# A Fourier-mixing network: products with 33 and 64 contraction rows are given all 128

## The chip, the cores and the metric

The kernel runs on one core of one Trainium2 chip. The metric is the device time of one execution in microseconds, the median of several runs, and a profile was taken of one execution. TensorE (PE) does matrix products, VectorE (DVE), ScalarE (ACT) and GpSimd (POOL) the element-wise work, and SyncE (SP) issues the transfers (DMA). A product loads one operand as weights (PEld, LDWEIGHTS) and streams the other; the number of *rows* of a product is the number of partitions over which it contracts, its *columns* are the partitions of its output, and its width is the number of elements streamed.

## The reference

Eight batches of 576 tokens with 512 features. Attention makes x, a block with a two-dimensional Fourier transform mixes it and runs a feed-forward net, and a second net with token shift follows.

```python
# attention, per batch and head
q_s = softmax(q, axis=-1); k_s = softmax(k, axis=2)
x = einsum(q_s, einsum(k_s, v))                 # 8 x 576 x 512
# first net
X = np.fft.fft(np.fft.fft(x, axis=1), axis=2)
u = x + np.real(X)
un = (u - mean(u)) / np.sqrt(var(u) + 1e-06)
x = u + np.maximum(un @ w_ch1, 0.0) @ w_ch2
# second net
x_prev = shifted by one token
k = np.maximum((mu_k*x + (1-mu_k)*x_prev) @ w_k, 0.0)
v = k * k @ w_v
out = sigmoid((mu_r*x + (1-mu_r)*x_prev) @ w_r) * v
```

## The kernel before

**Stages.** The tokens of all batches form one sequence of 4608, cut into nine blocks of 512. For block `i` the products of the first net run as `mm1` (L938, into the PSUM tile `h`) and `mm2` (L959, into `acc`), with each f32 operand split into a high and a low f16 part. Between them, `side()` takes one step each of two strands: `front_x` (attention of the next batches) and `front_y` (the transform and the normalization of the next batches). So the transform of batch 0 runs before the first block, the transforms of batches 1 to 7 run between the main products of the blocks, on the same PE queue, and end at about 855 us; after the ninth block the second net runs (L1002, L1015, L1030). A scheduler sets the order in which each engine's instructions are queued; each engine runs its queue in order.

**The transform** of a batch is two stages of products in `fp32r`, each operand split in a high and a low part.

In stage 1 (L469 to L488) six groups of products form `yh` and `yl`: for i = 0, 1, 2 and e = 0 (cosine) or 1 (sine). `JT` gives the output columns: 128, 128 and then 64 (e = 0) or 32 (e = 1). A group is six products with 128 rows (L477); the three groups with e = 0 end in a seventh (L480), whose operands `x6` and `alt` have 33 partitions. Only partitions 0 and 32 hold data: the high and the low part of one row.

In stage 2 (`stage2`, L493) a group is six products with 128 rows (L497) and a last one (L501). The three groups a batch with the cosine table `csh`, `csl` have one more before the last, L499, over the first 64 partitions. In the third slice of `yh` partitions 0 to 63 hold the high part of the remaining rows and 64 to 127 their low part; `csl[:, 2]` is zero from partition 64 on. The last product has 128 rows with the cosine table and 96 with the sine table `ssh`.

So a batch has three products with 33 rows (two with 128 columns, one with 64) and three with 64 rows, 24 of each in the kernel. After each L480 group ACT and DVE take the result to `yh` and `yl`; after each cosine group of stage 2 ACT copies it to `pc` (L507) or `sd` (L517).

**The start.** `first_constants` loads the table `alt` (33 x 290) through a staging tile `st` of tag `pc`, of which there is one buffer, and copies it by ACT to `alt` and to `x6` (L147). The buffer held 1/512 before, which ACT reads at L142. Attention of batch 0 follows on the same queues; its maximum (DVE, L304), the exponentials of q (ACT, L327) and k (ACT, L334) and the products with v (PE, L345) are named below. The f16 weights are decoded meanwhile on DVE (L194, L195).

Of the kernel before, what the change touches and what calls it, by code (L numbers as in the profile page):

```python
# [8 lines left out]
F32 = mybir.dt.float32  # L9
F32R = mybir.dt.float32r  # L10
# [11 lines left out]
NS = 290  # L22
# [21 lines left out]
def net(ctx, tc, q, k, v, w1, w2, mu_k, mu_r, w_k, w_v, w_r, ce_d, se_d, cs_d, ss_d, alt_d, id_d, out):  # L44
    nc = tc.nc
# [13 lines left out]
    def bank(tag, bufs, shape=(128, 512)):  # L59
        return ps.tile(list(shape), F32, tag=tag, name=tag, bufs=bufs)  # L60
# [3 lines left out]
    def aside(first, strand):  # L64


        turn_of[0] += 1
        if not first:
            return bank(f"side{turn_of[0] % 2 if done_block[0] < 0 else strand}", 1)
        x = turn_of[0] % 6  # L70
        return bank(f"side{x // 3}", 1) if x in (0, 3) else bank(f"acc{(1, 2, 4, 5).index(x)}", 1)

    mm = nc.tensor.matmul
# [19 lines left out]
    fc = front.enter_context(tc.tile_pool(name="fc", bufs=1))  # L93
    fw = front.enter_context(tc.tile_pool(name="fw", bufs=1))
# [25 lines left out]
    csl = fc.tile([128, 3, NS], F32R, name="csl")  # L120
    ssh = fc.tile([128, 3, NS], F32R, name="ssh")
    ssl = fc.tile([128, 3, NS], F32R, name="ssl")
    alt = fc.tile([33, NS], F32R, name="alt")
    x6 = fc.tile([33, NS], F32R, name="x6")
    kvbd = [fc.tile([128, 2, 129], F32, name=f"kvbd{x}") for x in range(2)]

    def load_constants():
# [9 lines left out]
    def first_constants():  # L137
        st = fw.tile([128, NS], F32, tag="pc", name="st")[:, 0:128]
        nc.vector.memset(st, 1.0 / DM)
        nc.vector.memset(one, 1.0)  # L140
        nc.gpsimd.memset(wsc[:, 7:8], 1e-6)
        nc.scalar.activation(out=onesr, in_=st, func=AF.Copy)  # L142
        nc.sync.dma_start(out=ident, in_=id_d)
        st = fw.tile([128, NS], F32, tag="pc", name="st")[0:33]
        nc.sync.dma_start(out=st, in_=alt_d)
        for x in (alt, x6):
            nc.scalar.activation(out=x, in_=st, func=AF.Copy)  # L147
        for x in kvbd:
            nc.gpsimd.memset(x, 0.0)
# [136 lines left out]
    def attention(b):  # L286
        tt = nc.vector.tensor_tensor
        for hf in range(2):
            if (b, hf) == (0, 0):
                load_k(b, 0)  # L290
                load_q(b, 0)
                first_constants()
                load_k(b, 1)
                load_v(b, 0)
                load_q(b, 1)
                load_v(b, 1)
# [119 lines left out]
    def transform(b):  # L416
# [50 lines left out]
        yh = fw.tile([128, 3, NK + 256], F32R, tag="yh", name="yh")  # L467
        yl = fw.tile([128, 3, NK + 256], F32R, tag="yl", name="yl")
        for i in range(3):  # L469
            for e, (ch, cl, n0, n1) in enumerate(((ceh, cel, 0, NK), (seh, sel, NK, NK + 256))):  # L470
                j0, n = JT[e][i]
                js = slice(j0, j0 + n)
                pt = aside(b == 0, 1)[0:n, 0:n1 - n0]
# [19 lines left out]
        def stage2(cols, ch, cl):  # L493
            pt = aside(b == 0, 1)[:, 0:NS]
            for i in range(2):
                for a, c in ((yh, ch), (yh, cl), (yl, ch)):
                    mm(out=pt, lhsT=a[:, i, cols], rhs=c[:, i, :], start=(i == 0 and c is ch and a is yh), stop=False)  # L497
            if ch is csh:
                mm(out=pt, lhsT=yh[0:64, 2, cols], rhs=cl[0:64, 2, :], start=False, stop=False)  # L499
            n = 128 if ch is csh else 96  # L500
            mm(out=pt, lhsT=yh[0:n, 2, cols], rhs=ch[0:n, 2, :], start=False, stop=True)  # L501
            return pt

        for g in range(2):
            pp = stage2(slice(1 + 128 * g, 129 + 128 * g), csh, csl)
            pc = fw.tile([128, NS], F32, tag="pc", name="pc")
            nc.scalar.activation(out=pc, in_=pp, func=AF.Copy)  # L507
            yield 1
            qq = stage2(slice(NK + 128 * g, NK + 128 * g + 128), ssh, ssl)
            tt(out=sd[:, g, 1, :], in0=pc, in1=qq, op=ALU.subtract)  # L510
            tt(out=sd[:, g, 0, :], in0=pc, in1=qq, op=ALU.add)
            yield 1
        tt(out=u[:, 0:2, 0:289], in0=u[:, 0:2, 0:289], in1=sd[:, :, 1, 0:289], op=ALU.add)
        tt(out=u[:, 0:2, S - 1:288:-1], in0=u[:, 0:2, S - 1:288:-1], in1=sd[:, :, 0, 1:288], op=ALU.add)
        pp = stage2(slice(0, 128), csh, csl)
        nc.scalar.activation(out=sd[0:1, 0], in_=sd[0:1, 1], func=AF.Copy)
        ma = nc.scalar.activation(out=sd[0:1, 1], in_=pp[0:1, None, :].to_broadcast([1, 2, NS]), func=AF.Copy)  # L517
# [472 lines left out]
    for i, (t0, n) in enumerate(blocks):  # L990
# [7 lines left out]
        for x, (o, m) in enumerate(subs):  # L998
            pt = bank("h", 2)
# [145 lines left out]
def build(inputs):  # L1145
    import concourse.bacc as bacc

    nc = bacc.Bacc("TRN2", target_bir_lowering=False, num_devices=1, dynamic_dma_scratch_size=1024)
    arrays, args = {}, []
    for name, a in [*_laid_out(inputs).items(), *_constants().items()]:  # L1150
        arrays[f"in_{name}_dram"] = a
        args.append(nc.dram_tensor(f"in_{name}_dram", a.shape, mybir.dt.from_np(a.dtype), kind="ExternalInput").ap())
    b, _, s, _ = inputs["q"].shape
    args.append(nc.dram_tensor("out_0_dram", (b * s, DM), F32, kind="ExternalOutput").ap())
    with tile.TileContext(nc, schedule_with_timeline_sim=True) as tc:
        net(tc, *args)
    return nc, arrays
# [9 lines left out]
```

## Time and profile before

| | us |
|---|---|
| median of 3 runs | 1571.76 (1570.62 to 1573.12) |
| the profiled execution | 1570.43 |
| its span, first to last instruction | 1568.7 |
| PE busy with products | 1459.4 (93%) |
| DVE busy | 945.9 (60%) |
| ACT busy | 649.5 (41%) |
| POOL busy | 234.9 (15%) |

The span is the time between the first and the last instruction of the profiled execution, and 1.7 us of its time lie around it. Products overlap in PE's pipeline: each one's duration reaches into the next one's, so what a product takes of the queue is read from the difference of two starts, not from its duration. The granted clock is the share of TensorE's full clock (2.4 GHz) that it was given in a stretch: 1.00, or 0.50 for 1.2 GHz; a stretch of both shows a value between.

### The profile page before, as it was taken

How to read it: one execution, taken by the hardware profiler on the slowest of the kernel's cores; microseconds unless marked ns; L12 is line 12 of the kernel's file. 1: busy time of each engine (PE TensorE's matmuls, PEld its weight loads, DVE VectorE, ACT ScalarE, POOL GpSimd, SP SyncE). 2: the span in 40 equal slices, each digit the busy share in tenths (PEclk: the TensorE clock that was granted, in tenths of full speed). 3: DMA queues.
4: the chain of work that ended last, by engine and by line, in shares of the span. 5: the costliest groups of instructions: out<-in, count | busy, mean ns of one | idle time of the engine just before them, and what ended most of it. 6: DMA issues, size and time to landing. Idle time of an engine off the chain costs nothing.

```text
span 1568.7 us, 18474 instructions
## 1 busy us (share of the span) xinstructions
PE 1459.4 (93%) x7123; PEld 759.2 (48%) x7123; DVE 945.9 (60%) x1635; ACT 649.5 (41%) x1183; POOL 234.9 (15%) x183
## 2 busy tenths in 40 slices
PE   4547995899999999999999999997999999999999
PEld 3435653555555555555555444443444444444444
DVE  8897738646567585664542364777886556554423
ACT  5677523323334233332321243435665435543322
POOL 2653402111001020110200200221100000000000
PEclk9668996999999999999999999998999999999999
DMA  7651202101112111111011035431111011100000
GB/s 298 195 152 48 80 16 74 48 32 48 42 48 75 35 46 42 48 36 40 1 37 41 32 116 182 133 99 63 54 55 54 1 54 54 55 1 28 27 27 28
DMA packets 43988, 99.81 MB, mean 64 GB/s; under 512 B 5723, under 2 KB 12156, under 8 KB 43900
## 3 DMA queue, kind: packets, MB, share of 16 engines
q1 hardware_dynamic: 43900, 98.63, 18.6%
q8 instruction: 56, 0.92, 0.3%
q14 instruction: 32, 0.26, 0.1%
HBM read 79.73 MB, written 18.87 MB: 63 GB/s over the span
## 4 chain that ended last, share of the span: by engine, by line
PE 75%; DVE 16%; ACT 4%; issue 2%; DMA 2%; POOL 1%; DVEq 0%; ACTq 0%; POOLq 0%; SPq 0%
PE h L938 22%; PE acc L959 22%; PE h L1015 11%; PE acc L1030 8%; PE h L1002 3%; DVE aa L782 2%; PE side L497 2%; PE side L477 2%; DVE wr L195 2%; PE side L398 1%; PE side L345 1%; DVE wr L194 1%; DVE x L784 1%; ACT aa L778 1%; DVE m L304 1%
## 5 line engine op out<-in xcount | busy, mean ns | idle before, releaser
L938 PE MATMUL h<-unh,wr 128*128 128x512 f16 (+1 forms) x1216 | 372.5, 370 | 7.0 <-ACT wr L232 3.6
L959 PE MATMUL acc<-hh,wr 128*128 128x512 f16 x1152 | 367.0, 380 | 0.0
L938 PEld LDWEIGHTS <-wr 128*128 128x128 f16 x1824 | 175.8, 98 | 197.5 <-issue 11.8
L959 PEld LDWEIGHTS <-wr 128*128 128x128 f16 x1728 | 164.7, 98 | 192.3 <-issue 3.5
L938 PE MATMUL h<-unl,wr 128*128 128x512 f16 (+1 forms) x608 | 225.1, 371 | 2.0 <-DVE unl L640 2.0
L959 PE MATMUL acc<-hl,wr 128*128 128x512 f16 x576 | 218.7, 380 | 0.0
L944 DVE SCALAR_TENSOR_TENSOR hl<-h,hh 128x512 f16<-128x512 f32 x144 | 99.1, 689 | 172.0 <-ACT hh L943 171.6
L1030 PE MATMUL acc<-wvh,kke 128*128 128x512 f16 x576 | 181.3, 379 | 0.1
L943 ACT ACTIVATE hh<-h 128x512 f16<-128x512 f32 x144 | 85.7, 596 | 217.4 <-PE h L938 217.2
L1015 PE MATMUL h<-x,wkh 128*128 128x512 f16 x576 | 171.5, 379 | 1.4 <-DVE aa L781 0.8
L1030 PEld LDWEIGHTS <-kke 128*128 128x128 f16 x864 | 84.3, 98 | 102.1 <-DVE kke L1022 0.6
L1020 ACT ACTIVATE kke<-kke 128x512 f32<-128x512 f32 x72 | 45.1, 626 | 159.8 <-DVE kke L1019 159.5
L1019 DVE SCALAR_TENSOR_TENSOR kke<-h,rg 128x512 f32<-128x512 f32 x72 | 49.5, 689 | 99.4 <-PE h L1015 99.3
L1030 PE MATMUL acc<-wvl,kke 128*128 128x512 f16 x288 | 109.2, 379 | 0.0
L1015 PE MATMUL h<-x,wkl 128*128 128x512 f16 x288 | 109.2, 379 | 0.0
L1002 PE MATMUL h<-wrh,x 128*128 128x512 f16 x288 | 90.5, 387 | 10.7 <-ACT x L783 7.3
L1015 PEld LDWEIGHTS <-wkh 128*128 128x128 f16 x576 | 55.8, 98 | 67.7 <-issue 1.7
L1022 DVE TENSOR_TENSOR kke<-kke 128x512 f16<-128x512 f32 x72 | 49.6, 690 | 59.7 <-ACT kke L1021 59.2
L1002 PEld LDWEIGHTS <-x 128*128 128x128 f16 x432 | 42.9, 99 | 64.9 <-issue 8.8
L782 DVE SCALAR_TENSOR_TENSOR aa<-y,ms,aa 128x512 f32<-128x512 f32 x72 | 62.8, 882 | 4.8 <-ACT aa L778 3.0
L574 POOL TENSOR_TENSOR sq<-u 128x128 f32<-128x128 f32 (+7 forms) x15 | 24.5, 1634 | 255.7 <-DVE u L519 110.1
L783 ACT ACTIVATE x<-aa 128x512 f16<-128x512 f32 x72 | 43.9, 623 | 42.0 <-PE h L1015 19.0
(323 smaller groups left out, 2194.9 us busy)
## 6 DMA issues: line engine op xcount, KB each, us to landing
vt<-in_v_dram SPq DMA_DIRECT2D x16, 650.0 KB, 5.0
kt<-in_k_dram SPq DMA_DIRECT2D x16, 576.0 KB, 3.8
qt<-in_q_dram SPq DMA_DIRECT2D x16, 576.0 KB, 3.8
out_dram<-oo SPq DMA_DIRECT2D x36, 256.0 KB, 2.1
y<-yT SPq DMA_DIRECT2D x8, 1026.0 KB, 5.0
raw<-in_w_dram SPq DMA_DIRECT2D x16, 512.0 KB, 4.3
words<-in_w_dram SPq DMA_DIRECT2D x16, 512.0 KB, 4.4
raw<-in_w_k_dram SPq DMA_DIRECT2D x32, 256.0 KB, 3.4
```

What stands on the lines that cost most here:

```text
L782: nc.vector.scalar_tensor_tensor(out=a, in0=y[:, t, 1:n + 1], scalar=mu[:, w, 0, t:t + 1], in1=a, op0=ALU.mult, op1=ALU.add)
L783: nc.scalar.activation(out=h[:, t, 0:n], in_=a, func=AF.Copy)
L938: mm(out=pt[:, o:o + m], lhsT=a, rhs=c[:, t, o:o + m], start=(t == z == 0), stop=(t == 3 and z == 2))
L943: ma = nc.scalar.activation(out=hh[:, 0:n], in_=pt[:, 0:n], func=AF.Relu)
L944: mv = nc.vector.scalar_tensor_tensor(out=hl[:, 0:n], in0=pt[:, 0:n], scalar=0.0, in1=hh[:, 0:n], op0=ALU.max, op1=ALU.subtract)
L959: mm(out=acc[x][:, 0:n], lhsT=a, rhs=c[:, 0:n], start=(f == z == 0), stop=(f == NF - 1 and z == 2))
L1002: mm(out=pt[0:m, :], lhsT=a[:, t, o:o + m], rhs=c[:, t, :], start=(t == 0 and a is rh and c is wrh), stop=(t == 3 and a is rl))
L1015: mm(out=pt[:, 0:n], lhsT=a[:, t, fs], rhs=c[:, t, 0:n], start=(t == 0 and a is wkh and c is kh), stop=(t == 3 and a is wkl))
L1019: nc.vector.scalar_tensor_tensor(out=kr[:, 0:n], in0=pt[:, 0:n], scalar=0.0, in1=G[:, 0:n], op0=ALU.max, op1=ALU.mult)
L1020: nc.scalar.activation(out=kr[:, 0:n], in_=kr[:, 0:n], func=AF.Square, scale=2.0 ** -76)
L1022: nc.vector.tensor_tensor(out=l2[:, 0:n], in0=kr[:, 0:n], in1=h2[:, 0:n], op=ALU.subtract)
L1030: mm(out=acc[x][0:m, :], lhsT=a[:, o:o + m], rhs=c[:, f, :], start=(f == 0 and a is h2 and c is wvh), stop=(f == NFK - 1 and a is l2))
```

## The change

`alt` and `x6` become tiles of 128 partitions. Their staging tile is set to zero over all 128 partitions by DVE before the table is loaded into its first 33, and the two ACT copies take all 128 partitions, so that the added rows are zero in both operands. The product of L499 takes all 128 partitions of `yh` and `csl` in place of the first 64; the rows that come in meet the zeros of `csl`. What is computed is the same, and so is the number of products.

```diff
-    alt = fc.tile([33, NS], F32R, name="alt")
-    x6 = fc.tile([33, NS], F32R, name="x6")
+    alt = fc.tile([128, NS], F32R, name="alt")
+    x6 = fc.tile([128, NS], F32R, name="x6")
...
-        st = fw.tile([128, NS], F32, tag="pc", name="st")[0:33]
-        nc.sync.dma_start(out=st, in_=alt_d)
+        st = fw.tile([128, NS], F32, tag="pc", name="st")
+        nc.vector.memset(st, 0.0)
+        nc.sync.dma_start(out=st[0:33], in_=alt_d)
...
             if ch is csh:
-                mm(out=pt, lhsT=yh[0:64, 2, cols], rhs=cl[0:64, 2, :], start=False, stop=False)
+                mm(out=pt, lhsT=yh[:, 2, cols], rhs=cl[:, 2, :], start=False, stop=False)
```

Line numbers after the change are two higher from L147 on. The order of the queues differs at two places only; from batch 1 on each engine's queue is the same.

The first is the start. On SP, the queue that issues the transfers, this stands before the change:

```order
L255 DMA kt<-in_k_dram 128x1152
L266 DMA qt<-in_q_dram 128x1152
L143 DMA ident<-in_ident_dram 128x128
L255 DMA kt<-in_k_dram 128x1152
L145 DMA st<-in_alt_dram 33x290
L261 DMA vt<-in_v_dram 128x1300
L266 DMA qt<-in_q_dram 128x1152
```

and this after it:

```order
L257 DMA kt<-in_k_dram 128x1152
L268 DMA qt<-in_q_dram 128x1152
L144 DMA ident<-in_ident_dram 128x128
L257 DMA kt<-in_k_dram 128x1152
L263 DMA vt<-in_v_dram 128x1300
L147 DMA st<-in_alt_dram 33x290
L268 DMA qt<-in_q_dram 128x1152
```

The table's transfer has moved behind that of the first v. On ACT the start of the queue before is:

```order
L877 ACT_TABLE_LOAD
L142 ACTIVATE onesr<-st 128x128
L147 ACTIVATE alt<-st 33x290
L147 ACTIVATE x_97<-st 33x290
L327 ACTIVATE qt<-qt 128x1152
L334 ACTIVATE kt<-kt 128x1152
```

and after (the shapes are those of the output):

```order
L879 ACT_TABLE_LOAD
L143 ACTIVATE onesr<-st 128x128
L329 ACTIVATE qt<-qt 128x1152
L149 ACTIVATE alt<-st 128x290
L149 ACTIVATE x_97<-st 128x290
L336 ACTIVATE kt<-kt 128x1152
```

The two copies of the table now stand between the exponential of q and that of k. On DVE one MEMSET of `st` is new, right behind those of L139 and L140.

The second place is stage 2 of batch 0 on PE. The two tiles are those of its first two cosine groups; before:

```order
L497 MATMUL acc_382<-csl,yh 128x290
L497 MATMUL acc_382<-csh,yl 128x290
L499 MATMUL acc_382<-csl,yh 128x290
L497 MATMUL side_403<-csh,yh 128x290
L497 MATMUL side_403<-csl,yh 128x290
...
L499 MATMUL side_403<-csl,yh 128x290
L501 MATMUL acc_382<-csh,yh 128x290
L501 MATMUL side_403<-csh,yh 128x290
```

and after:

```order
L499 MATMUL acc_383<-csl,yh 128x290
L499 MATMUL acc_383<-csh,yl 128x290
...
L499 MATMUL side_404<-csh,yl 128x290
L501 MATMUL acc_383<-csl,yh 128x290
L503 MATMUL acc_383<-csh,yh 128x290
L501 MATMUL side_404<-csl,yh 128x290
L503 MATMUL side_404<-csh,yh 128x290
```

The first group's added product has moved behind the six of the second group, next to the group's last one.

## Rows read from the trace of the kernel before

**Rows 1.** Windows: length, busy PE, PEld, DVE, ACT, POOL; granted clock, DMA share, GB/s.

```profile
60.00:115.00 55.00, 31.69 (x118) 24.33 (x118) 49.72 (x76) 38.42 (x88) 33.34 (x23) 0.72 0.57 172
182.00:246.80 64.80, 64.78 (x347) 38.34 (x345) 30.41 (x52) 21.70 (x39) 8.09 (x7) 1.00 0.13 46
246.80:297.70 50.90, 28.38 (x117) 17.14 (x118) 42.37 (x65) 21.44 (x38) 15.85 (x9) 0.73 0.22 73
297.70:1067.00 769.30, 768.88 (x3828) 401.98 (x3828) 439.18 (x770) 256.83 (x488) 99.42 (x85) 1.00 0.18 58
1067.00:1569.00 502.00, 484.69 (x2256) 218.63 (x2254) 281.46 (x513) 230.10 (x381) 30.61 (x22) 0.99 0.11 38
```

**Rows 2.** L480 and L499 by line: count, duration in ns, first and last start, shapes.

```profile
L480 PE MATMUL side<-alt,x x22: 328/382/383, 67.3 to 819.0; 33*128 33x258 f32 x15, 33*64 33x258 f32 x7
...
L499 PE MATMUL side<-csl,yh x22: 393/394/400, 78.4 to 854.5; 64*128 64x290 f32 x22
```

**Rows 3.** Windows of L480's products alone (columns as in rows 1).

```profile
246.80:297.70 50.90, 0.76 (x2) 0.37 (x2) 0.73 0.22 73
297.70:1067.00 769.30, 5.80 (x16) 2.61 (x16) 1.00 0.18 58
```

**Rows 4.** Windows of L499's products alone.

```profile
297.70:1067.00 769.30, 7.10 (x18) 3.29 (x18) 1.00 0.18 58
```

**Rows 5.** Timeline of PE at a 64-row product: start, duration, what.

```profile
842.34 0.29 PE L497 MATMUL side<-csh,yl 128*128 128x290 f32 x1
842.56 0.39 PE L499 MATMUL side<-csl,yh 64*128 64x290 f32 x1
842.88 0.40 PE L501 MATMUL side<-csh,yh 128*128 128x290 f32 x1
843.12 0.39 PE L959 MATMUL acc<-hh,wr 128*128 128x512 f16 x1
```

**Rows 6.** Timeline of PE at a 96-row product.

```profile
848.48 0.29 PE L501 MATMUL side<-ssh,yh 96*128 96x290 f32 x1
848.61 0.39 PE L959 MATMUL acc<-hh,wr 128*128 128x512 f16 x1
```

**Rows 7.** Timeline of PE at a 33-row product with 128 columns.

```profile
806.39 0.28 PE L477 MATMUL side<-ceh,eh 128*128 128x258 f32 x1
...
806.62 0.28 PE L477 MATMUL side<-ceh,el 128*128 128x258 f32 x1
806.83 0.38 PE L480 MATMUL side<-alt,x 33*128 33x258 f32 x1
807.14 0.39 PE L938 MATMUL h<-unl,wr 128*128 128x512 f16 x1
```

**Rows 8.** Timeline of PE at a 33-row product with 64 columns.

```profile
818.83 0.28 PE L477 MATMUL side<-ceh,el 128*64 128x258 f32 x1
819.04 0.33 PE L480 MATMUL side<-alt,x 33*64 33x258 f32 x1
819.30 0.39 PE L938 MATMUL h<-unl,wr 128*128 128x512 f16 x1
```

**Rows 9.** Timeline of ACT at the start; idle before and releaser in brackets.

```profile
8.99 0.45 ACT L147 ACTIVATE alt<-st 33x290 fp32r<-33x290 f32 x1 [6.67 <-DMA st<-in_alt_dram]
...
10.85 1.16 ACT L327 ACTIVATE qt<-qt 128x1152 f32<-128x1152 f32 x1 [1.07 <-POOL qt L326]
14.15 1.16 ACT L334 ACTIVATE kt<-kt 128x1152 f32<-128x1152 f32 x1 [2.15 <-DVE kt L333]
```

**Rows 10.** The tile vt in the first 25 us: its three transfers.

```profile
DMA to landing us min/median/max: 6.2/7.3/9.4
```

**Rows 11.** Timeline of DVE at the start.

```profile
4.71 1.89 DVE L304 TENSOR_REDUCE m<-kt 128x256 f32<-128x1024 f32 x1 [3.58 <-DMA kt<-in_k_dram]
```

**Rows 12.** Chain of waits at block 1: start, duration, what.

```profile
297.75 4.44 PE h L938 x12
...
326.40 2.59 PE h L938 x12
```

## The prediction

> **What bounds the kernel now.** I read the windows first, cut where the chain of waits changes engine [rows 1]. From 297.7 to 1067 us PE is busy 768.88 of 769.30 us while DVE is busy 439 and ACT 257: every microsecond that a product holds PE longer than it must is a microsecond of the result. The same holds from 182 to 246.8 us (64.78 of 64.80). It does not hold in two stretches. From 60 to 115 us, where the transform of batch 0 runs, PE has 31.7 of 55.0 us and DVE, which also decodes weights there, 49.7. From 246.8 to 297.7 us PE has 28.4 of 50.9 us and DVE 42.4: block 1 waits for the normalization of batch 1. After 1067 us there is no transform any more, and PE is again busy 485 of 502 us.
>
> Then I placed the changed products. There are 22 of each kind on the `side` tiles, and two more of each on `acc`, in batch 0; they run from 67.3 to 819.0 us (33 rows) and from 78.4 to 854.5 us (64 rows) [rows 2]. Three of each kind belong to batch 0 and so to the DVE-bound stretch; three of each belong to batch 1, in the stretch from 182 to 246.8 us. Two with 33 rows lie in the stretch where PE waits, and 16 [rows 3] and 18 [rows 4] in the long PE-bound one. So 19 products with 33 rows and 21 with 64 rows stand where PE is the limit.
>
> **What each costs in the queue.** A product's duration covers its latency too; the queue is read from starts. Around a 64-row product the starts are 842.34, 842.56, 842.88 and 843.12: three steps of 0.22, 0.32 and 0.24 us, 0.78 in all [rows 5]. An ordinary product of the same width takes 0.13 to 0.14 us of the queue, and this holds for the one with 96 rows: the next starts 0.13 us after it, though that is an f16 product of another width [rows 6]. So it is not fewer rows as such that cost time: 96 do not and 64 do. Three ordinary steps are 0.40 us. A 64-row product thus costs 0.38 us beside its own work, spread over the step into it, the step out of it, and the step after that, where the next operand is loaded late.
>
> Around a 33-row product with 128 columns the starts are 806.62, 806.83, 807.14, 0.52 us for two steps; the two ordinary steps from 806.39 to 806.62 take 0.23, and 0.24 with rounding [rows 7]. That is 0.28 us. With 64 columns it is 818.83 to 819.30, 0.47 us, so 0.23 us [rows 8].
>
> The Trainium skill has two rules that pull apart here. "TensorE: Matmul & The Clock Gate" (section "Why this matters for your kernels") says that one product over 32 rows takes as long as one over 128. By it alone nothing is saved and the sum is 1571.8 us. "TensorEngine Tiling (Array Packing)" (section "Key Properties") says that a change of the tiling mode drains the engine. The rows side with the second: the 96-row product would still use the whole array, and only the 33- and 64-row ones change the mode, into it and out again. By that rule the sum below stands.
>
> **The change, term by term.** The changed products keep their widths, 258 and 290, and their columns. After the change they are of the same form as their neighbours, so I give them an ordinary step.
> - 64 rows: 21 x 0.38 = 8.0 us.
> - 33 rows, 128 columns: batch 1 and batches 3 to 7 have two each, 12 x 0.28 = 3.4 us.
> - 33 rows, 64 columns: batches 1 to 7 have one each, 7 x 0.23 = 1.6 us.
> - The third step after a 33-row product. Before an f16 product nothing is late; before another f32 product it may be by up to 0.10 us, as in the third step of rows 5 (0.24 against 0.14). The bounds are 0 and 12 x 0.10 = 1.2 us. About half of the 12 are followed by such a product, so I take 0.5 us.
> - Batch 0, six products, some 1.9 us of PE time by the same prices: nothing, since DVE's work covers it. If that cover were gone it would all come through. The move of the 64-row product behind the second group shifts only a result that DVE takes later.
> - The two in the waiting stretch, some 0.6 us of PE time: nothing.
> - The zeroing of `st`: DVE idles for 3.58 us before L304 at 4.71 [rows 11], and one small MEMSET fits in there. Without that cover it would cost its duration, less than the 0.45 us that ACT needs for as wide a tile [rows 9].
> - The two ACT copies keep their width of 290 elements, 0.45 us each [rows 9]. They now come behind the exponential of q, which ends at 10.85 + 1.16 = 12.01 us, and must be done before that of k at 14.15. Room is 2.14 us, need 0.9. Nothing, if the table is there by 13.2 us.
>
> The sum is 8.0 + 3.4 + 1.6 + 0.5 = 13.5 us. The profiled execution took 1570.43 us, so it would take 1556.9. The median of the runs lies 1.3 us above that execution; I predict **1558.3 us**.
>
> Does the gain reach the end? Batch 1's share, about 2.2 us, comes before the wait of block 1. Its last product releases the DVE and ACT work that fills that wait, so the whole stretch should move up with it. From 297.7 us on nothing else holds PE. Whatever the second net needs at 1067 us is produced behind PE's products, so it moves too. I see no stall that takes the place of the lost time: DVE has 330 us to spare in the long stretch.
>
> **Rivals.**
> - *Only one kind gains.* The 64-row product follows and precedes others of its own group, the 33-row one brings operands of other tiles. If something else than the rows makes the 33-row ones late, the gain is 8.0 us and the time 1563.8; if the 64-row ones, 5.5 us and 1566.3. Against it: both show the same two late steps, 0.21 or 0.22 and then 0.26 to 0.32 us.
> - *Nothing gains.* The zero rows cost what the switch cost before, or the time is lost again in the wait of block 1 and after it: 1571.8. Only batch 1's share could be lost there (then 1560.5); for the rest the 768.88 of 769.30 us speak against it [rows 1]. This is where the rule of the Trainium skill on "Why this matters for your kernels" ("TensorE: Matmul & The Clock Gate") would end; the 0.78 against 0.40 us speak against it.
> - *Slower.* The table's transfer is issued behind that of the first v. It was there at 8.99 us before [rows 9]; v's transfers took 6.2 to 9.4 us [rows 10]. ACT would wait at the copies with the exponential of k, the k v products on PE and all of batch 0 behind it. From 13.2 us on each microsecond of delay is one of the result, if DVE has no slack to cover it. To turn the gain into a loss it would have to land after 13.2 + 13.5 + 3, near 30 us. A start at about 3.6 us plus 9.4 is 13.0, so I expect nothing or some tenths; a time of 1575 and more would need a queue unlike any in this trace.
> - *The clock.* The first 12 products after block 1's wait took 4.44 us where 12 take 2.59 later [rows 12], as a stretch of some 3.5 us at half clock makes it. Moving that stretch by two microseconds may spare or repeat such a loss of 1.85 us, or shift another in the waiting stretch (granted 0.73 on the mean there [rows 1]). This makes the range, not a rival of its own.
>
> **How the numbers follow.** My forecast has a chance of 0.86, with the variants that batch 1's share is lost or the clock differs; one kind alone 0.08; nothing 0.04; slower 0.02. The forecast's own spread is 1558.3 less 1.2 for the third steps and batch 0's share or a spared clock loss of 1.9, so about 1554.5 below; above, 2.2 for batch 1 and 1.9 for the clock give 1562.4. To leave out no more than 2 in 10 I go to 1564, which takes in the case that only the 64-row products gain. A measurement of this kernel can tell about 0.2%, 3.1 us, from no change: faster 0.94, same 0.04, slower 0.02.
>
> **What would show it.** In the profile after, the starts around L501 (the former L499) should be 0.13 to 0.14 us apart throughout, and around L482 (the former L480) 0.12; the durations fall from 0.39 and 0.38 to about 0.30 and 0.28. PE's busy time should fall by some 13 to 15 us, and the stretch of block 1's wait should begin about 2 us earlier and be as long. Were the steps short and the time unchanged, the gain went into a wait; were the steps still long, the reason is not the rows. At the start, the copies of the table should be done before k's exponential, still at about 14.15 us. What would make the prediction wrong is a wait for the table, a new stretch at half clock in the long PE-bound stage, or a step that stays late because of the 64 columns.

## The result

The changed kernel takes 1558.85 us (median of 6 runs, 1557.30 to 1559.51); the kernel before took 1571.12 us in 6 runs of the same kind (1569.57 to 1573.12). The ratio is 0.9916 with an interval of 0.9905 to 0.9927. The medians lie 12.3 us apart. 1558.3 was predicted, a gain of 13.5 us from the 1571.76 us of the first three runs. The profiled execution took 1559.01 us, its span is 1557.2 us, 11.5 us less than before.

The first view is PE's timeline at the three places shown of before: the widened 64-row product (L501, formerly L499), the widened 33-row product with 128 columns (L482, formerly L480) and the one with 64 columns. The columns are start, duration, what.

```profile
843.15 0.29 PE L499 MATMUL side<-csh,yl 128*128 128x290 f32 x1
843.28 0.29 PE L501 MATMUL side<-csl,yh 128*128 128x290 f32 x1
843.41 0.29 PE L503 MATMUL side<-csh,yh 128*128 128x290 f32 x1
843.55 0.60 PE L961 MATMUL acc<-hh,wr 128*128 128x512 f16 x2
...
796.77 0.28 PE L479 MATMUL side<-ceh,el 128*128 128x258 f32 x1
796.89 0.28 PE L482 MATMUL side<-alt,x 128*128 128x258 f32 x1
797.01 0.39 PE L940 MATMUL h<-unl,wr 128*128 128x512 f16 x1
...
808.70 0.28 PE L479 MATMUL side<-ceh,el 128*64 128x258 f32 x1
808.82 0.28 PE L482 MATMUL side<-alt,x 128*64 128x258 f32 x1
808.94 0.39 PE L940 MATMUL h<-unl,wr 128*128 128x512 f16 x1
```

Three steps around the 64-row product took 0.78 us [rows 5] and take 0.40 now (843.15 to 843.55). Two steps around the 33-row ones took 0.52 [rows 7] and 0.47 [rows 8] and take 0.24 now. Every changed product has become an ordinary one, the one with 64 columns too.

By line, the 22 of each kind on `side` tiles show it in their durations, which were 393 to 400 ns and 328 to 383 ns [rows 2]:

```profile
L501 PE MATMUL side<-csl,yh x22: 293/294/302, 79.6 to 843.3; 128*128 128x290 f32 x22
...
L482 PE MATMUL side<-alt,x x22: 276/280/286, 69.1 to 808.8; 128*128 128x258 f32 x15, 128*64 128x258 f32 x7
```

The windows from batch 1 on, cut at the same instructions as those of before (length; busy PE, PEld, DVE, ACT, POOL; clock, DMA share, GB/s):

```profile
184.20:247.20 63.00, 62.94 (x346) 37.95 (x344) 30.51 (x52) 21.69 (x39) 8.10 (x7) 1.00 0.13 47
247.20:296.90 49.70, 27.73 (x117) 16.94 (x118) 42.40 (x65) 21.60 (x39) 15.43 (x9) 0.76 0.21 75
296.90:1055.50 758.60, 757.50 (x3828) 399.73 (x3828) 439.21 (x770) 256.60 (x488) 99.41 (x85) 1.00 0.18 59
1055.50:1557.50 502.00, 484.63 (x2256) 218.63 (x2254) 281.48 (x513) 230.10 (x381) 30.61 (x22) 0.99 0.11 38
```

The stretch that ends with batch 1 became 1.8 us shorter (64.8 to 63.0; 2.2 had been forecast), the wait of block 1 behind it 1.2 us (50.9 to 49.7), the long PE-bound stretch 10.7 us (769.3 to 758.6), with the same counts of instructions; the second net kept its 502 us [rows 1]. PE's busy time in the long stretch fell by 11.4 us (768.88 to 757.50). The stretch itself gave back 0.7 us less, because PE now waits for 1.1 us in it, and waited for 0.4 before. These are the two places, with the idle time and what ended it in brackets; before, PE idled 0.11 and 0.26 us there:

```profile
584.34 0.66 PE L381 MATMUL side<-ident,qt 128*128 128x128 f32 x4 [0.46 <-DVE qTl L376]
...
648.68 0.50 PE L565 MATMUL side<-hl,onesr 128*128 128x512 f32 x1 [0.56 <-ACT hl L563]
```

So a small part of the lost steps came back as waits for DVE and ACT.

The sum of these is 13.7 us, and 11.5 came out: the execution was 2.2 us late before batch 1 began (184.2 in place of 182.0). ACT's timeline at the start:

```profile
10.96 1.16 ACT L329 ACTIVATE qt<-qt 128x1152 f32<-128x1152 f32 x1 [8.63 <-POOL qt L328]
12.03 0.43 ACT L149 ACTIVATE alt<-st 128x290 fp32r<-128x290 f32 x1
12.36 0.43 ACT L149 ACTIVATE x<-st 128x290 fp32r<-128x290 f32 x1
14.27 1.16 ACT L336 ACTIVATE kt<-kt 128x1152 f32<-128x1152 f32 x1 [1.48 <-DVE kt L335]
```

and DVE's, where the MEMSET is the new one:

```profile
2.45 0.30 DVE L146 MEMSET st<- 128x290 f32 x1 [1.33 <-ACT onesr L143]
4.82 1.89 DVE L306 TENSOR_REDUCE m<-kt 128x256 f32<-128x1024 f32 x1 [2.07 <-DMA kt<-in_k_dram]
```

The table was there when the exponential of q ended, its copies ran at once, and ACT then idled 1.48 us until k's turn. k's exponential starts 0.12 us later than before [rows 9], and DVE's first reduction already 0.11 us later [rows 11], because k landed that much later. So the moved load cost nothing here.

### The profile page after: what moved, and what is told of

Read it like the earlier page. It is cut to its first block, busy times and chain, and to the rows that moved or that the text cites. A ratio compares the mean times of both kernels' runs of the same rounds, so it can differ in the third digit from the quotient of the medians.

```text
span 1557.2 us, 18476 instructions
## 1 busy us (share of the span) xinstructions
PE 1446.1 (93%) x7123; PEld 759.1 (49%) x7123; DVE 946.3 (61%) x1636; ACT 649.5 (42%) x1183; POOL 234.3 (15%) x183
## 4 chain that ended last, share of the span: by engine, by line
PE 73%; DVE 16%; ACT 5%; DMA 2%; issue 1%; POOL 1%; SPq 0%; ACTq 0%; DVEq 0%; POOLq 0%
PE h L940 21%; PE acc L961 21%; PE h L1017 11%; PE acc L1032 8%; PE h L1004 3%; DVE aa L784 2%; PE side L499 2%; PE side L479 1%; DVE wr L197 1%; PE side L400 1%; PE side L347 1%; DVE wr L196 1%; DVE x L786 1%; ACT aa L780 1%; DMA kt<-in_k_dram 1%
## 5 line engine op out<-in xcount | busy, mean ns | idle before, releaser
L1024 DVE TENSOR_TENSOR kke<-kke 128x512 f16<-128x512 f32 x72 | 49.6, 690 | 59.7 <-ACT kke L1023 59.2
```

Source lines behind the costliest of these rows:

```text
L1024: nc.vector.tensor_tensor(out=l2[:, 0:n], in0=kr[:, 0:n], in1=h2[:, 0:n], op=ALU.subtract)
```

## The experiments

**One kind of product alone.** The first kernel widens the 64-row product and leaves the rest, the start too:

```diff
-                mm(out=pt, lhsT=yh[0:64, 2, cols], rhs=cl[0:64, 2, :], start=False, stop=False)
+                mm(out=pt, lhsT=yh[:, 2, cols], rhs=cl[:, 2, :], start=False, stop=False)
```

> Only the 64-row product is widened; the 33-row ones and the start stay. Mode theory (a product over 33 or 64 rows makes PE switch into another form and out again, 0.38 us per 64-row product, 21 of them where PE is the limit): 8.0 us less than the kernel before, about 1563.1. Rival (only the 33-row ones gained, for another reason than the rows): no change, about 1571. The steps around L499 should be 0.13 to 0.14 us, those around L480 stay 0.21 and 0.31.

Measured: 1564.21 us, ratio 0.9951 (0.9939 to 0.9963), by which it is 7.7 us faster (5.8 to 9.6). The second kernel is the changed one with this line as it was before, so that only the 33-row products are widened:

> Only the 33-row products are widened, with the start as in the changed kernel. Mode theory: 5.5 us less than before, about 1565.6; together with the run that widens only the 64-row product the two gains should sum to that of the whole change, 12 to 13 us. Rival (only the 64-row ones gained): about 1571.

Measured: 1567.78 us, ratio 0.9975 (0.9967 to 0.9984), 3.9 us less (2.5 to 5.2; single times from 1565.0 to 1569.9). Both kinds gain, so the rival that only one does is out. 7.7 and 3.9 add up to 11.6, against 12.3 for the whole. The 64-row term is what the steps said, 8.0; the 33-row one came out 1.6 us under my 5.5, which lies just outside its interval.

**How many rows are enough.** The changed kernel with 96 rows in place of 128 for the one and 65 for the other:

```diff
-    alt = fc.tile([128, NS], F32R, name="alt")
-    x6 = fc.tile([128, NS], F32R, name="x6")
+    alt = fc.tile([65, NS], F32R, name="alt")
+    x6 = fc.tile([65, NS], F32R, name="x6")
...
-                mm(out=pt, lhsT=yh[:, 2, cols], rhs=cl[:, 2, :], start=False, stop=False)
+                mm(out=pt, lhsT=yh[0:96, 2, cols], rhs=cl[0:96, 2, :], start=False, stop=False)
```

> The products with 64 and 33 rows are given 96 and 65 rows instead of 128. Mode theory (what counts is whether the product needs more than half of the array's rows): all the gain of the change, about 1559, and ordinary steps of 0.13 and 0.12 us. Rival (the cost grows with the rows left out, or only the full 128, or a multiple of 32, is free): the 65-row products stay late by up to 0.28 us each, up to 5.5 us less gain, about 1564.

Measured: 1558.68 us, ratio 0.9920 (0.9908 to 0.9932), the time of the changed kernel. Its PE timeline:

```profile
796.54 0.28 PE L479 MATMUL side<-ceh,el 128*128 128x258 f32 x1
796.66 0.28 PE L482 MATMUL side<-alt,x 65*128 65x258 f32 x1
796.79 0.39 PE L940 MATMUL h<-unl,wr 128*128 128x512 f16 x1
...
843.07 0.30 PE L501 MATMUL side<-csl,yh 96*128 96x290 f32 x1
843.20 0.29 PE L503 MATMUL side<-csh,yh 128*128 128x290 f32 x1
```

The steps are 0.12 to 0.13 us with 65 rows, as with 128. So the price does not grow with the rows left out. It is there with 64 rows at the one product and gone with 65 at the other; the two counts were not tried at one and the same product.

**The start as before.** Both products widened, the table loaded and copied as in the kernel before, the tiles zeroed by GpSimd:

```diff
         for x in (alt, x6):
-            nc.scalar.activation(out=x, in_=st, func=AF.Copy)
+            nc.gpsimd.memset(x.bitcast(F32), 0.0)
+            nc.scalar.activation(out=x[0:33], in_=st, func=AF.Copy)
```

> Both products are widened, but the table is loaded and copied over 33 partitions as before; GpSimd zeroes both tiles ahead of the copies. In the profile of the changed kernel batch 1 began about 2.2 us later than before. If the moved load and the copies behind the exponential of q cost that: about 1556.7, and the first main product starts where it does in the kernel before (123.2 us). If it is the clock of that execution, or the work of batch 0 itself: about 1558.9, no difference that can be told from the changed kernel.

Measured: 1560.57 us (1557.34 to 1563.31), ratio 0.9929 (0.9916 to 0.9942): not less than with the moved load. In its profile the first main product starts even later, at 122.58 us, and at 121.35 us in the kernel before (the 123.2 us of the expectation is a later product of the same block). So the moved load is not what made the first 182 us longer. These are the first main products of the kernel before, the changed one and this one; each row is from another kernel's timeline:

```profile
121.35 0.58 PE L938 MATMUL h<-unh,wr 128*128 128x256 f16 x2 [0.56 <-ACT unh L639]
```
```profile
122.45 0.59 PE L940 MATMUL h<-unh,wr 128*128 128x256 f16 x2 [0.55 <-ACT unh L641]
```
```profile
122.58 0.58 PE L939 MATMUL h<-unh,wr 128*128 128x256 f16 x2 [0.56 <-ACT unh L640]
```

With only 64 rows, only 33 rows, and 96 and 65 rows it starts at 122.03, 121.58 and 122.32 us. The moved load is in the changed kernel and in the last two of these, and one of them is the earliest but one of the six. In these six the clock granted in the first 130 us goes with the order: it is 0.71 in the three late ones (122.45, 122.58 and 122.32) and 0.75 to 0.77 in the others. Two more of the kernels below break this rule. The one with additional 64-row products apart had 0.72 and is early. The one with additional products in batch 4 alone had 0.73 and is the latest of all, though each engine's queue up to there is that of the kernel before. The first main product of each:

```profile
121.46 0.59 PE L940 MATMUL h<-unh,wr 128*128 128x256 f16 x2 [0.56 <-ACT unh L641]
```
```profile
122.76 0.59 PE L940 MATMUL h<-unh,wr 128*128 128x256 f16 x2 [0.55 <-ACT unh L641]
```

At the last products ahead of batch 1's stretch that second kernel is 2.5 us behind the kernel before; the kernel before, and then it:

```profile
181.15 0.70 PE L317 MATMUL side<-m,one 128*128 128x256 f32 x2 [0.74 <-DVE m L316]
```
```profile
183.67 0.70 PE L317 MATMUL side<-m,one 128*128 128x256 f32 x2 [1.40 <-DVE m L316]
```

The changed kernel runs them at 183.45 us. So an execution with an unchanged start can be as late as that of the changed kernel, and the 2.2 us are no proof of a cost of the change. That the clock is their cause is not shown; what sets them stays open.

**One change of form or one price per product.** The kernel before with one more 64-row product in each of the 24 cosine groups, times a table of zeros. First right behind the one that is there:

```diff
                 mm(out=pt, lhsT=yh[0:64, 2, cols], rhs=cl[0:64, 2, :], start=False, stop=False)
+                mm(out=pt, lhsT=yh[0:64, 2, cols], rhs=ssl[0:64, 2, :], start=False, stop=False)
```

> The kernel before, with a second 64-row product right behind each of the 64-row ones (times a table of zeros, so it adds nothing to the sum). Mode theory: the switch is paid once for the pair, and the second product adds an ordinary step of 0.13 to 0.14 us: 21 x 0.135 = 2.8 us, about 1573.9. Rival (each product with few rows pays for itself): 21 x (0.135 + 0.38) = 10.8 us, about 1582.

Then three products ahead of it, and at that place with 128 and with 32 rows:

```diff
                     mm(out=pt, lhsT=a[:, i, cols], rhs=c[:, i, :], start=(i == 0 and c is ch and a is yh), stop=False)
+                if ch is csh and i == 0:
+                    mm(out=pt, lhsT=yh[0:64, 2, cols], rhs=ssl[0:64, 2, :], start=False, stop=False)
```

> The same additional 64-row product of zeros, but between two 128-row products of its group, three products ahead of the one that is there. Mode theory: it pays a switch of its own, 21 x (0.135 + 0.38) = 10.8 us, about 1582. Rival (each product pays for itself): also 1582, but then the pair should cost the same; the difference between the two runs tells.

> The same additional product at the same place with 128 rows: the price of the product alone. Both theories: 21 x 0.135 = 2.8 us, about 1573.9, and steps of 0.13 to 0.14 us.

> The same additional product at the same place with 32 rows. Mode theory, if each form but the full one costs the same to enter and to leave: about 1582, with steps of 0.22, 0.32 and 0.24 us as around the 64-row product. Rival (the cost grows with the rows left out): more than 0.38 us of switching per product, 1584 or later.

Measured, against the same runs of the kernel before (1571.71 us):

| additional product | us | ratio (interval) | us more |
|---|---|---|---|
| 64 rows, in a pair | 1572.42 | 1.0010 (1.0000 to 1.0019) | 1.6 (0.0 to 3.0) |
| 64 rows, apart | 1579.71 | 1.0056 (1.0041 to 1.0071) | 8.8 (6.4 to 11.2) |
| 128 rows, apart | 1571.97 | 1.0006 (0.9996 to 1.0016) | 0.9 (-0.6 to 2.5) |
| 32 rows, apart | 1580.86 | 1.0061 (1.0042 to 1.0081) | 9.6 (6.6 to 12.7) |

These four kernels do not have the kernel before's order of queues: with the additional products the scheduler ordered DVE, ACT and PE anew in many places from batch 1 on, and in nearly the same way in all four. One place is DVE in the wait of block 1, before and then with 128 rows apart:

```profile
295.74 1.36 DVE L326 TENSOR_TENSOR qt<-qt,st 128x1152 f32<-128x1152 f32 x1
297.01 1.28 DVE L944 SCALAR_TENSOR_TENSOR hl<-h,hh 128x512 f16<-128x512 f32 x2
```
```profile
292.76 1.36 DVE L326 TENSOR_TENSOR qt<-qt,st 128x1152 f32<-128x1152 f32 x1
...
296.85 1.29 DVE L946 SCALAR_TENSOR_TENSOR hl<-h,hh 128x512 f16<-128x512 f32 x2
```

Before, L326 ran right ahead of the instruction that block 1 waits for; in the four kernels it runs earlier, while DVE has to wait for GpSimd anyway. Their wait of block 1 took 48.1 to 49.6 us, where it took 50.9 [rows 1]; on the other hand PE waits 1.3 us in each of them between 663 and 668 us, ahead of L383. So the columns against the kernel before hold the price of the products together with that of another order, and the four are best compared with one another.

In a pair the 64-row product costs like the 128-row one, which has no change of form (1572.42 and 1571.97 us). Apart it costs 1579.71 less 1571.97, 7.7 us for 21 products or 0.37 us each, against the 0.38 of the prediction. So what is paid is the change of form, not the product with few rows. 32 rows cost like 64: their single times overlap (1577.6 to 1582.3 us, and 1578.5 to 1580.8). PE's timeline at the pair, at the 64-row product apart, and at the one with 32 rows:

```profile
856.81 0.29 PE L497 MATMUL side<-csh,yl 128*128 128x290 f32 x1
857.03 0.40 PE L499 MATMUL side<-csl,yh 64*128 64x290 f32 x1
857.26 0.29 PE L500 MATMUL side<-ssl,yh 64*128 64x290 f32 x1
857.49 0.40 PE L502 MATMUL side<-csh,yh 128*128 128x290 f32 x1
857.72 0.60 PE L960 MATMUL acc<-hh,wr 128*128 128x512 f16 x2
```
```profile
862.08 0.29 PE L497 MATMUL side<-csh,yl 128*128 128x290 f32 x1
862.31 0.39 PE L499 MATMUL side<-ssl,yh 64*128 64x290 f32 x1
862.63 0.40 PE L497 MATMUL side<-csh,yh 128*128 128x290 f32 x1
862.87 0.29 PE L497 MATMUL side<-csl,yh 128*128 128x290 f32 x1
```
```profile
863.60 0.29 PE L497 MATMUL side<-csh,yl 128*128 128x290 f32 x1
863.82 0.39 PE L499 MATMUL side<-ssl,yh 32*128 32x290 f32 x1
864.14 0.40 PE L497 MATMUL side<-csh,yh 128*128 128x290 f32 x1
864.38 0.29 PE L497 MATMUL side<-csl,yh 128*128 128x290 f32 x1
```

Four steps of the pair take 0.91 us; four ordinary ones would take 0.54. The difference is 0.37, the same as around a single 64-row product. The 128-row product adds steps of 0.14 us in its trace, which make 2.9 us for 21; the time shows 0.9, with an interval that ends at 2.5. The other order of the queues can be the reason for these 2 us (in its profile the wait of block 1 took 48.7 us), but no run has the order without the products.

**Where the cover ends.** Twelve additional 64-row products of zeros, four to each cosine group and each between two 128-row ones, first in batch 0 alone and then in batch 4 alone:

```diff
                     mm(out=pt, lhsT=a[:, i, cols], rhs=c[:, i, :], start=(i == 0 and c is ch and a is yh), stop=False)
+                    if ch is csh and b == 0 and (a is yh):
+                        mm(out=pt, lhsT=yh[0:64, 2, cols], rhs=ssl[0:64, 2, :], start=False, stop=False)
```

> The kernel before, with twelve additional 64-row products of zeros in batch 0 alone, each between two 128-row products, so that each switches for itself: 12 x (0.135 + 0.38) = 6.2 us of PE time at full clock, in the stretch where DVE has 49.7 of 55.0 us. If DVE's work covers PE there, as the prediction had it: the steps are late in the trace and the time stays, 1571 to 1573. Rival (PE's products of batch 0 lie on the path): about 1578.

> The same twelve additional products in batch 4 alone, in the stretch where PE is busy 768.88 of 769.30 us: all 6.2 us show, about 1578. Rival (the feed-forward blocks have slack that takes some of it): less than half, under 1575.

Measured: in batch 4 1580.13 us, ratio 1.0049 (1.0035 to 1.0063), 7.7 us more (5.5 to 9.9): all of the 6.2. In batch 0 1574.82 us, ratio 1.0023 (1.0013 to 1.0032), 3.6 us more (2.0 to 5.0): between the two expectations. DVE's timeline there, and then that of the kernel before at the same instruction, which takes the first cosine group's result:

```profile
86.10 0.46 DVE L512 TENSOR_TENSOR sd<-pc,acc 128x290 f32<-128x290 f32 x1 [4.12 <-ACT pc L509]
```
```profile
81.55 0.44 DVE L510 TENSOR_TENSOR sd<-pc,acc 128x290 f32<-128x290 f32 x1
```

Before, DVE came from the decoding of weights without a pause; with the twelve products it waited 4.12 us for ACT's copy of PE's result. In that kernel part of these steps ran at half clock (1.2 GHz; the granted clock from 84 to 88 us is 0.50), so that PE lost more than 6.2 us there. Its PE timeline:

```profile
86.04 0.61 PE L499 MATMUL acc<-ssl,yh 64*128 64x290 f32 x1
86.57 0.61 PE L497 MATMUL acc<-csl,yh 128*128 128x290 f32 x1
87.11 0.61 PE L499 MATMUL acc<-ssl,yh 64*128 64x290 f32 x1
```

In the kernel before ACT copied that result to `pc` from 79.2 us on, for 0.41 us, so it lay ready for 2.0 us when DVE came to it. So DVE's work does cover PE in batch 0, but by some two microseconds, not by all that PE idles there. For a change that takes PE time away it makes the gain there nothing, as predicted; one that adds as much as this is paid for what exceeds the cover.

## Why the prediction was right

**The bound.** At my prices the 16 products with 33 rows and 18 with 64 rows in the long stretch from 297.7 us on are 18 x 0.38 + 10 x 0.28 + 6 x 0.23 = 11.0, and 11.4 with the share of the third steps. PE's busy time there fell by 11.4 us, and the stretch gave back 10.7. The 0.7 us between are the waits shown above: the prediction saw no stall that takes the place of the lost time, and there is a small one. All five kernels with widened products have it; their PE waits 0.9 to 1.9 us in that stretch, where 0.4 stood. The dose in batch 4 shows the same from the other side: 6.2 us of steps came out as 7.7 (5.5 to 9.9). Its queues too were ordered anew around batch 4; in its profile the time from block 1's first products to those of the second net grew by 5.3 us.

**The price of a 64-row product.** 0.38 us each, read from three steps. The run with these alone (7.7 us, 8.0 forecast) and the 64-row product apart against the 128-row one apart (0.37) both hold.

**The price of a 33-row product.** The steps in the trace have become 0.24 us where 0.52 and 0.47 were, as forecast. The third steps, of which I took 0.5 by estimate, can be read from the traces of the kernel before and the changed one. An f32 product follows six of the twelve with 128 columns and one of the seven with 64; its step fell from 0.17 to 0.11 us in five cases, from 0.21 to 0.11 and from 0.24 to 0.13 in the two others, 0.5 in all. Before an f16 product the third step is 0.23 us in both kernels. By time the term is smaller, 3.9 us (2.5 to 5.2) where 5.5 stood. In the profile of the kernel with only these products widened PE's busy time in the long stretch fell by 4.4 us (764.50 in place of 768.88), where the prices give 4.5, but the stretch became only 3.5 us shorter (765.80 in place of 769.30): the same waits again. They make up part of the 1.6 us; the rest is of the size by which single executions differ, and stays open.

**What was put at nothing.** Batch 0 gave nothing that shows: none of the five kernels with widened products reached its first main product before 121.35 us. Its cover has a limit that the prediction did not give. The zeroing took 0.30 us in an idle time of DVE. The table's copies ran at 12.03 us, in the room between the two exponentials; the rival that they would come late is out. The two 33-row products in the wait of block 1 were put at nothing, and that stretch became 1.2 us shorter. In the other four kernels with widened products it took 50.1 to 52.3 us, so the 1.2 us are of the size by which executions differ.

**The clock.** The half-clock run of twelve products after block 1's wait came again, at 296.91 us, 4.44 us long as in [rows 12], so nothing was spared there. The loss came at the start instead, 2.2 us in the profiled execution. The range allowed 1.9 for a loss by the clock; whether this was one is not shown.

**The signs and the number.** The steps and the durations came as named, and PE's busy time fell by 13.3 us (1459.4 to 1446.1). The wait of block 1 did not begin 2 us earlier and last as long: it began 0.4 us later and was shorter. That the time lies within 0.6 us of the forecast is in part luck. The two PE-bound stretches lost 13.2 us of PE's busy time, close to the 13.5 of the sum; what then took 2.2 us at the start and 0.7 in waits, and gave back 1.2 in the wait of block 1, was not forecast. And the gain is 12.3 us and not 13.5; the later runs of the kernel before put its median 0.6 us lower than the one that the forecast started from. Two figures of the prediction do not follow from its own prices: batch 1's share is 1.9 us by them, 2.1 with the third steps, and not 2.2 (1.8 came), and 1558.3 less 1.2 and 1.9 is 1555.2, not 1554.5.

The Trainium skill's page "TensorEngine Tiling (Array Packing)" (section "Key Properties") says that changing the tiling mode, not just the tile, drains the engine. The pair agrees, with 0.37 us for one excursion, whether it holds one product or two. "TensorE: Matmul & The Clock Gate" (section "Why this matters for your kernels") has a product over 32 rows take as long as one over 128. The runs agree only for the product itself, here one over 64 rows: the second of the pair added 0.13 us. Around a lone one it leaves out the two changes of form, which here cost nearly three times the product.

## What to carry to other kernels

Price a product in a dense PE queue by the differences of starts over three steps, into it, out of it and one further, since the cost of a neighbour of another form is spread over all three. Where a product over 64 rows or fewer stands alone among full ones on a busy PE, pad its operands with zeros to more than 64 rows, or put such products next to each other so that the change is paid once. Ask first where PE is the limit: the same products gave nothing where DVE's work sets the pace. Where an experiment adds instructions, compare the order of the queues too: here four kernels were ordered anew, and only their differences from one another gave the price.

## What the runs showed of the hardware that was not expected

The excursion falls into two equal changes. At the pair the steps are 0.22, 0.23, 0.23 and 0.23 us where 0.135 is ordinary: each change, in or out, delays the first product of the new form by 0.09 us and the one behind it by 0.10. This second delay depends on the first product of the new form: behind an f16 one it is nothing (807.14 to 807.37 us before, and 797.01 to 797.24 in the changed kernel), behind the f32 ones of L379 and L383 it is 0.05 to 0.06. That is why a 33-row product ahead of an f16 one costs 0.28 us and not 0.38. A lone 64-row product gets the second delay of the one change and the first of the other at once, so its step out is 0.32. The weight loads show a part of it. Before the change, they ran 0.11 us ahead of the product among equal ones and began with it at the 33-row one:

```profile
806.51 0.19 PEld L477 LDWEIGHTS side<-ceh,el 128*128 128x128 f32 x1
806.83 0.18 PEld L480 LDWEIGHTS side<-alt,x 33*128 33x128 f32 x1
```

The products started at 806.62 and 806.83 [rows 7].

At half clock the alternating steps of the dose in batch 0 took 0.53 to 0.54 us (86.04, 86.57, 87.11), against 0.24 for an ordinary step at that clock (73.10 and 73.34 in the kernel before, in batch 0): a change costs 0.30 us there and 0.19 at full clock. Fewer columns cost nothing that shows: the widened product with 64 columns has ordinary steps of 0.12 us on both sides, the one out of it into a product with 128 columns.
